# An attention and feed-forward kernel: bias loads of chunks 1 to 3 issued by GpSimd instead of the sync engine

## The chip, the cores and the metric

The kernel runs on one core of a Trainium2 chip. The metric is device time in microseconds for one launch. A core has a matrix engine (TensorE, PE in the profile; its weight loads are PEld), VectorE (DVE), ScalarE (ACT), GpSimd (POOL) and a sync engine (SP) that only issues transfers. Each engine works off its own instructions in program order and waits on semaphores for the others. Transfers between HBM and on-chip memory are started by an instruction on SP, ACT or POOL and then run on 16 shared transfer engines.

## What is computed

Attention with a learned position bias for 4 batches, 8 heads, 576 positions and head size 64, then a layer norm and a feed-forward block of width 2048 on the concatenated heads:

```python
scores = scale * np.matmul(q, k.transpose(0, 1, 3, 2))
x = (psi_rel / psi_i)[..., None]            # from positions alone
bias = np.maximum(x @ w1 + b1, 0.0) @ w2    # one 576 x 576 map per head
scores = scores + bias.transpose(2, 0, 1)[None, :, :, :]
attn = softmax(scores);  a = np.matmul(attn, v)       # heads side by side
xn = (a - mu) / np.sqrt(var + 1e-06) * g_ln
out = a + np.maximum(xn @ w_ch1, 0.0) @ w_ch2
```

## The kernel before, in words

The 576 query positions are cut into four chunks of 128 rows (c = 0 to 3) and a tail of 64 (c = 4). One **unit** is the attention of one batch, one chunk and one head (in a tail unit, two heads); there are 144 units, in the order of the list `ORD` (line 213). That list keeps units of one chunk together, since the four batches share a chunk's bias: chunk 0 up to unit 39, tails in units 40 to 47, chunk 1 in units 48 to 79, chunk 2 in 80 to 111, chunk 3 in 112 to 143.

The bias is computed on the chip in 36 groups of 16 positions (`bias_relu`, `bias_mm`), copied by ScalarE into a tile `ev`, and written to a buffer in HBM, `nb0` to `nb4`, one for each chunk (line 211). The writes of the first twelve groups (the tail and chunk 0) go out on POOL, those of the other 24 on SP. Once all groups of a chunk are written, eight tiles `ldb` of 128 x 576, one for each head, are loaded back (line 326); each is then used by all four batches.

A step `u` of the main loop (line 861) runs `softmax1(u)`: VectorE adds bias and scores and finds the row's extreme (L434), ScalarE takes the exponential (L438) and a scaled half-precision copy (L443). `softmax2(u - 1)` makes the rest of that value (L462, L464), and SP issues a transposing transfer of the result `e` into `pt` or `wend` (L470). `qk` makes the scores of two later units on PE (L391), `pv` multiplies the transposed probabilities by the values (L480). Each finished tile goes through a layer norm: VectorE takes mean and variance (L567, L568), POOL the factor `rs` (L569, L570), ScalarE and VectorE the normalized tile (L596, L599), SP transposes it into `xT` (L601). The feed-forward work on PE (L709, L736), with ScalarE's and VectorE's `hh` (L714, L717), is spread between the units so that PE has work at every step.

`issue_loads(u)` (line 277) goes through a list of loads sorted by the unit that needs them, and issues those whose time has come and whose buffer is free by the program's counters. Keys `kf` (L291, 8 buffers) and queries `qf` (L304, L307, 3 buffers) and values `vf` (L313) are issued on POOL, the bias tiles `ldb` (9 buffers) on SP. The lead is set by two numbers for each kind, the offset in the list and `LOOK`:

```python
loads.append((u0 + (g if c == 4 else 2 * g) - 4, "k", (n, b, g)))
loads.append((u0 + 4 * hh - 3, "q", (b, c, hh)))
loads.append((u0 + h, "b", (seg[n], c, h)))
LOOK = {"k": 5, "q": 6, "b": 7, "v": 0}
```

So a bias tile may be loaded seven steps ahead, and a key tile is asked for 9 - 2g steps ahead of its visit's first unit; it is used 2g units into the visit.

The order on each engine is the order in which the program emits instructions, as a scheduler has arranged them. Transfers are counted on semaphores, eight for SP's queue and eight for POOL's, used in turn; a transfer that comes to a semaphore again first waits until the transfer eight before it has landed.

Of the kernel before, what the change touches and what calls it, by code (L numbers as in the profile page):

```python
# [22 lines left out]
def kernel(  # L23
# [13 lines left out]
    V, S, G, T, SY = nc.vector, nc.scalar, nc.gpsimd, nc.tensor, nc.sync  # L37
# [24 lines left out]
    def halves(t):  # L62
# [31 lines left out]
    nbias = [  # L94
        t[0:(128 if c < 4 else 64) * NH * PITCH].rearrange("(i h j) -> i h j", h=NH, j=PITCH)
        [:, :, 16:16 + SEQ] for c, t in enumerate(nflat)
    ]
# [40 lines left out]
    def after(ins, dep):  # L138
        if dep is not None:
            tc.add_manual_dep(ins.ins, dep.ins.name,  # L140
                              mybir.DependencyInfo(mybir.DependencyClass.Sync,
                                                   mybir.DependencyReason.DATA),
                              reason="pace")
# [133 lines left out]
    def issue_loads(u):  # L277
        wait = set()
        for item in list(loads):
# [5 lines left out]
            if kind == "k":  # L285
# [4 lines left out]
                raw = kp.tile([128, 2, HS], F32, tag="k", name="kf")  # L290
# [4 lines left out]
            elif kind == "q":  # L295
                if not qfree[0]:
                    wait.add(kind)
                    continue
                qfree[0] -= 1
                b, c, hh = key  # L300
                raw = qp.tile([128, 512], F32, tag="q", name="qf")
                if c < 4:
                    raw = raw.rearrange("p (a b) -> p a b", a=4)
                    ld = G.dma_start(out=raw, in_=q_main[b, c, :, 4 * hh:4 * hh + 4])  # L304
                else:
                    raw = raw.rearrange("p (a b) -> p a b", a=8)
                    ld = G.dma_start(out=raw, in_=q_tail[b])  # L307
                if gate_on[0] and (b, c) != ORD[0]:
                    gate.append(ld)
                qt[key] = raw  # L310
            elif kind == "v":
                raw = vp.tile([128, 640], F32, tag="v", name="vf")
                ld = G.dma_start(out=raw.rearrange("p (a b c) -> p a b c", a=2, b=5),  # L313
                                 in_=v_p[key[0], :, 2 * key[1]:2 * key[1] + 2])
                if ttri:
                    after(ld, ttri[max(ttri)])
                vraw[key] = raw
            else:
                _, c, h = key
                if not bfree[0] or mm_done[0] < gend[c]:  # L320
                    wait.add(kind)
                    continue
                bfree[0] -= 1
                raw = ldp.tile([128, SEQ], F32, tag="ld", name="ldb")
                if c < 4:
                    SY.dma_start(out=raw, in_=nbias[c][:, h, :])
                else:
                    SY.dma_start(out=raw[0:64], in_=nbias[4][:, 2 * h, :])
                    SY.dma_start(out=raw[64:128], in_=nbias[4][:, 2 * h + 1, :])
                bt[key] = raw  # L330
# [478 lines left out]
    for _ in range(2):  # L809
        load_w()  # L810
    issue_loads(-6)
    issue_loads(-5)
    V.memset(mhalf, -0.5)
    V.memset(one_sb, 1.0)
    V.memset(half4, 0.5)
    bias_setup()
    issue_loads(-4)
    for n in range(NP + 1):
        if n < NP:
# [172 lines left out]
```

## Time and profile before

| | us |
|---|---|
| median of 3 runs | 678.46 |
| lowest and highest of the runs | 678.29 and 684.29 |
| the profiled execution, whole | 679.99 |
| its span in the profile | 678.2 |
| PE busy | 647.7 (96%) |
| VectorE busy | 457.8 (68%) |
| ScalarE busy | 392.0 (58%) |
| POOL busy | 97.4 (14%) |
| mean granted PE clock | 0.985 of 2.4 GHz |

All times in the rows are microseconds from the start of the span, which is one execution. In rows in order of time the columns are start, duration, engine, line, operation, output<-input, count, and in brackets the idle time just before on that engine and what ended it. "POOLq", "SPq" are the queues of instructions that only issue transfers; a row that merges several (x2, x3) gives the time of them together. A wait for several semaphores is put down to the one that came last.

### The profile page before, as it was taken

To read this page: it belongs to the slowest core of one execution; us is meant where nothing else is said; L and a number is where in the kernel's file an instruction comes from. 1 tells how busy PE (TensorE), PEld (TensorE's weight loads), DVE (VectorE), ACT (ScalarE), POOL (GpSimd) and SP (SyncE) were. 2 spreads that over 40 slices of the span, in tenths; PEclk is the share of its full clock that TensorE was granted. 3 is DMA by queue.
4 is the path that set the end of the run, shared out by engine and by line. 5 is a ranking of instruction groups with operands and counts; after the bars stand their busy time and mean duration, and the time that the engine had idled before them with its cause. 6 is when DMAs were issued, how large, how long until landed. Compare 5 with 4: busy or idle time off the path is not lost.

```text
span 678.2 us, 19142 instructions
## 1 busy us (share of the span) xinstructions
PE 647.7 (96%) x7929; PEld 448.4 (66%) x7929; DVE 457.8 (68%) x1061; ACT 392.0 (58%) x777; POOL 97.4 (14%) x163
## 2 busy tenths in 40 slices
PE   6889996998999889999899999999999999999997
PEld 4447774676466666666667766666776677677775
DVE  6588999778757567686766575757576676766322
ACT  5565847478957447787764577576554455444110
POOL 5312321011000011111101110111011120000000
PEclk9989997899999999999899999999999999999999
DMA  8999885444659996868869789789996976744100
GB/s 312 294 404 331 307 294 161 143 91 115 143 122 148 223 246 156 173 156 164 172 149 239 134 183 181 136 197 181 201 200 144 166 153 125 121 98 87 33 16 17
DMA packets 186955, 117.24 MB, mean 173 GB/s; under 512 B 163956, under 2 KB 164084, under 8 KB 186868
## 3 DMA queue, kind: packets, MB, share of 16 engines
q1 hardware_dynamic: 177124, 81.00, 55.8%
q0 software_dynamic: 9600, 34.84, 16.6%
q8 instruction: 62, 1.02, 0.6%
q10 hardware_dynamic: 144, 0.18, 0.1%
q14 instruction: 25, 0.20, 0.1%
HBM read 60.51 MB, written 15.63 MB: 112 GB/s over the span
## 4 chain that ended last, share of the span: by engine, by line
PE 50%; DVE 0%; ACT 0%; issue 0%
PE hps L709 19%; PE y L736 18%; PE sps L391 6%; PE xps L480 6%; PE bps L181 1%; DVE v L369 0%; DVE x L747 0%; DVE e L462 0%; ACT e L443 0%; DVE x L516 0%; ACT t L438 0%; DVE e L464 0%
## 5 line engine op out<-in xcount | busy, mean ns | idle before, releaser
L709 PE MATMUL hps<-xT,w 128*128 128x128 f16 x3240 | 196.4, 220 | 5.8 <-DVE hh L717 2.6
L709 PEld LDWEIGHTS <-w 128*128 128x128 f16 x3240 | 184.6, 98 | 11.5 <-issue 5.2
L736 PE MATMUL y<-w,hh 128*128 128x512 f16 x810 | 189.1, 381 | 1.9 <-ACT hh L714 1.8
L438 ACT ACTIVATE t<-t,m 128x576 f32<-128x576 f32 x144 | 111.0, 771 | 132.8 <-DVE m L434 132.2
L736 PEld LDWEIGHTS <-hh 128*128 128x128 f16 x864 | 79.7, 98 | 90.6 <-ACT hh L714 3.3
L462 DVE SCALAR_TENSOR_TENSOR e<-t,e 128x512 f16<-128x512 f32 x120 | 82.8, 690 | 81.8 <-ACT e L443 81.5
L434 DVE CUSTOM_DVE_ANT_0 t<-sps,ldb 128x576 f32<-128x576 f32 x144 | 105.9, 753 | 31.4 <-PE sps L391 21.2
L391 PE MATMUL sps<-kf,qf 64*128 64x288 f32 (+1 forms) x640 | 96.6, 436 | 3.5 <-DVE m L434 3.5
L443 ACT ACTIVATE e<-t 128x576 f16<-128x576 f32 x120 | 80.8, 679 | 9.8 <-DMA pt<-e 3.5
L714 ACT ACTIVATE hh<-hps 128x512 f16<-128x512 f32 x72 | 42.0, 583 | 53.4 <-PE hps L709 47.9
L717 DVE SCALAR_TENSOR_TENSOR hh<-hps,hh 128x512 f16<-128x512 f32 x72 | 49.4, 687 | 34.0 <-ACT hh L714 33.5
L391 PEld LDWEIGHTS sps<-kf,qf 64*128 64x128 f32 (+1 forms) x640 | 48.2, 176 | 35.6 <-issue 17.5
L480 PEld LDWEIGHTS <-pt 128*128 128x128 f16 (+1 forms) x1456 | 49.3, 100 | 30.5 <-issue 24.9
L747 DVE SCALAR_TENSOR_TENSOR x<-y,ycs,x 128x512 f32<-128x512 f32 x58 | 43.4, 748 | 32.2 <-PE y L736 32.0
L480 PE MATMUL xps<-v,pt 128*128 128x64 f16 (+1 forms) x1456 | 59.0, 195 | 1.9 <-DMA pt<-e 1.1
L291 POOL DMA_DIRECT2D kf<-in_k_s_dram x56 | 31.1, 556 | 161.4 <-PE sps L391 114.3
L304 POOL DMA_DIRECT2D qf<-in_q_main_dram x32 | 18.5, 577 | 162.4 <-PE xps L480 82.6
L187 ACT ACTIVATE ev<-bps,cb_sb,par_sb 128x144 f32<-128x144 f32 (+27 forms) x48 | 26.0, 593 | 26.2 <-PE bps L181 26.0
L160 ACT ACTIVATE r<-psi_sb,par_sb 128x448 f32<-128x448 f32 (+23 forms) x72 | 39.7, 614 | 0.0
L569 POOL TENSOR_SCALAR rs<-mv 128x1 f32<-128x1 f32 x18 | 9.9, 549 | 146.3 <-DVE mv L568 138.3
L438 ACT ACTIVATION_READ_ACCUMULATOR t<-t,m 128x1 f32 x144 | 27.0, 188 | 0.0
L181 PE MATMUL bps<-r,nw_sb 128*32 128x448 f32 (+24 forms) x200 | 26.9, 494 | 0.0
(121 smaller groups left out, 641.4 us busy)
## 6 DMA issues: line engine op xcount, KB each, us to landing
kf<-in_k_s_dram POOLq DMA_DIRECT2D x56, 288.0 KB, 4.8
w<-in_w_ch_dram SPq DMA_DIRECT2D x22, 512.0 KB, 8.7
ldb<-nb SPq DMA_DIRECT2D x32, 288.0 KB, 4.5
qf<-in_q_main_dram POOLq DMA_DIRECT2D x32, 256.0 KB, 4.6
nb<-ev SPq DMA_DIRECT2D x24, 296.0 KB, 3.4
vf<-in_v_p_dram POOLq DMA_DIRECT2D x16, 320.0 KB, 7.5
out_dram<-x SPq DMA_DIRECT2D x18, 256.0 KB, 2.1
wend<-in_w_ch_dram SPq DMA_DIRECT2D x8, 512.0 KB, 4.8
```

Of the source, the lines that this page charges most:

```text
L160: S.activation(r[:, 0:n], psi_sb[:, 0:n], AF.Relu, bias=pr_sb[:, g4:g4 + 1], scale=1.0)
L391: m = T.matmul(out=o, lhsT=l, rhs=kk, start=True, stop=True, tile_position=(64 * hf, 64 * e))
L434: ttri[u] = V.tensor_tensor_reduce(out=halves(t), in0=ps[:, :, 0:HS], in1=halves(bias), scale=-0.125, scalar=3e38, op0=ALU.add, op1=ALU.mi ...
L438: S.activation(t, t, AF.Exp, bias=m, scale=-1.0, accum_out=l8[b, c][:, h:h + 1])
L443: S.activation(e16[:, 0:SEQ], t, AF.Copy, scale=E_SCALE)
L462: V.scalar_tensor_tensor(out=e16[:, 640:1152], in0=t[:, 0:512], scalar=E_SCALE, in1=e16[:, 0:512], op0=ALU.mult, op1=ALU.subtract)
L480: T.matmul(out=o, lhsT=p[:, m], rhs=v[:, j, a, :], start=(i == 0), stop=(i == len(ops) - 1))
L709: T.matmul(out=h[:, idx * n:idx * n + n], lhsT=w[:, wo + kk * 128:wo + kk * 128 + 128], rhs=xT[k][:, xo + kk, 0:n], start=(i == 0), stop=( ...
L714: S.activation(hh[:, 0], h, AF.Relu)
L717: V.scalar_tensor_tensor(out=hh[:, 1], in0=h, scalar=0.0, in1=hh[:, 0], op0=ALU.max, op1=ALU.subtract)
L736: T.matmul(out=yps[k][t], lhsT=hh[:, a, o:o + 128], rhs=w[:, wo:wo + 512], start=(f == f0 and i == 0), stop=(f == f1 - 1 and i == 2))
L747: V.scalar_tensor_tensor(out=x, in0=y, scalar=ycs[:, g:g + 1], in1=x, op0=ALU.mult, op1=ALU.add)
```

## The change

One line of `issue_loads`: which engine issues the load of a bias tile of chunks 1 to 3. Chunk 0's and the tails' stay on SP.

```diff
@@ issue_loads, kind "b"
                 raw = ldp.tile([128, SEQ], F32, tag="ld", name="ldb")
                 if c < 4:
-                    SY.dma_start(out=raw, in_=nbias[c][:, h, :])
+                    (G if c else SY).dma_start(out=raw, in_=nbias[c][:, h, :])
                 else:
                     SY.dma_start(out=raw[0:64], in_=nbias[4][:, 2 * h, :])
                     SY.dma_start(out=raw[64:128], in_=nbias[4][:, 2 * h + 1, :])
```

24 loads change their queue, eight for each chunk. PE, VectorE and ScalarE keep their instructions and their order. Below are the places where SP's and POOL's rows change. On SP, at chunk 1 (`nb_125` is that chunk's buffer in HBM; the first row is its last write; rows with - stand only in the kernel before):

```order
 L211 DMA nb_125<-ev 16x8x592
-L326 DMA ldb<-nb_125 128x576 x3
 L470 DMA_TRANSPOSE wend<-e_3098 128x9x128
 L470 DMA_TRANSPOSE pt<-e_3137 128x9x128
-L326 DMA ldb<-nb_125 128x576 x2
 L470 DMA_TRANSPOSE pt<-e_3223 128x9x128
 L470 DMA_TRANSPOSE pt<-e_3265 128x9x128
 L751 DMA out_dram<-x 128x512
-L326 DMA ldb<-nb_125 128x576 x2
 L470 DMA_TRANSPOSE pt<-e_3360 128x9x128
 L470 DMA_TRANSPOSE wend<-e_3423 128x9x128
```

The eight loads go, and the transposes follow the write directly. On POOL, at the same place, the rows with + stand only in the changed kernel:

```order
 L304 DMA qf<-in_q_main_dram 128x512
-L291 DMA kf<-in_k_s_dram 128x576 x3
+L291 DMA kf<-in_k_s_dram 128x576 x2
+L326 DMA ldb<-nb_125 128x576 x5
+L291 DMA kf<-in_k_s_dram 128x576
 L304 DMA qf<-in_q_main_dram 128x512
 L291 DMA kf<-in_k_s_dram 128x576
+L326 DMA ldb<-nb_125 128x576 x2
 L569 TENSOR_SCALAR rs<-mv 128x1
 L570 TENSOR_TENSOR rs<-rs,mhalf 128x1
+L326 DMA ldb<-nb_125 128x576
 L304 DMA qf<-in_q_main_dram 128x512
```

Five loads stand ahead of the third key load, two ahead of the layer norm's `rs`, one behind it. At chunks 2 and 3 it is four, then a query load, then three, `rs`, and one. The rows of POOL at chunk 1 again, with what each waits for (DMAHW and DMASW are the semaphores of SP's and of POOL's transfers, eight each):

```order
+L326 DMA ldb<-nb_125 128x576 [waits DMAHW3_49,DMAHW5_49,DMAHW1_49,DMAHW7_49,DMASW7_49,DVE_49]
+L326 DMA ldb<-nb_125 128x576 [waits DMAHW6_49,DMASW0_49,DVE_49]
+L326 DMA ldb<-nb_125 128x576 [waits DMAHW4_49,DMASW1_49,DVE_49]
+L326 DMA ldb<-nb_125 128x576 [waits DMAHW0_49,DMASW2_49,DVE_49]
+L326 DMA ldb<-nb_125 128x576 [waits DMASW3_49,DVE_49]
+L291 DMA kf<-in_k_s_dram 128x576 [waits DMASW4_49,PE_49]
+L304 DMA qf<-in_q_main_dram 128x512 [waits DMASW5_49,PE_49]
+L291 DMA kf<-in_k_s_dram 128x576 [waits DMASW6_49]
+L326 DMA ldb<-nb_125 128x576 [waits DMAHW2_49,DMASW7_49,DVE_49]
```

The first bias load waits for the writes of its chunk, and the sixth uses the same semaphore (DMASW7) as the first, so it waits until the first has landed.

## Rows read from the trace of the kernel before

**Rows 1.** Busy time, share of the span and instructions of each engine.

```profile
PE 647.7 (96%) x7929; PEld 448.4 (66%) x7929; DVE 457.8 (68%) x1061; ACT 392.0 (58%) x777; POOL 97.4 (14%) x163
```

**Rows 2.** Stretches: length, busy (count) PE, PEld, DVE, ACT, POOL; clock, DMA share, GB/s.

```profile
232.00:255.00 23.00, 20.74 (x359) 15.05 (x352) 14.81 (x37) 11.17 (x23) 2.45 (x4) 1.00 1.15 225
255.00:330.00 75.00, 75.00 (x978) 51.04 (x978) 52.53 (x126) 57.49 (x119) 10.93 (x18) 1.00 0.77 168
330.00:340.00 10.00, 8.00 (x113) 6.30 (x110) 8.77 (x19) 7.21 (x13) 2.11 (x3) 0.83 0.83 148
340.00:620.00 280.00, 280.00 (x3606) 196.44 (x3605) 185.41 (x434) 158.78 (x313) 33.74 (x55) 1.00 0.80 160
```

**Rows 3.** PE in order of time, 216 to 260 us: the rows after idle time.

```profile
225.41 2.84 PE L709 MATMUL hps<-xT,w 128*128 128x128 f16 x48 [1.28 <-DVE hh L717]
...
236.10 0.63 PE L480 MATMUL xps<-v,wend 128*64 128x64 f16 x28 [0.53 <-DMA wend<-e]
...
250.19 2.17 PE L709 MATMUL hps<-xT,w 128*128 128x128 f16 x36 [1.30 <-DVE hh L717]
...
253.47 0.63 PE L480 MATMUL xps<-v,pt 128*64 128x64 f16 x28 [0.43 <-DVE x L543]
```

**Rows 4.** SP's queue in order of time: chunk 1's last bias write on; chunk 2.

```profile
223.53 0.58 SPq L211 DMA_DIRECT2D nb<-ev  x1
228.76 1.28 SPq L326 DMA_DIRECT2D ldb<-nb  x3
230.21 2.01 SPq L470 DMA_TRANSPOSE wend<-e  x1
232.39 2.62 SPq L470 DMA_TRANSPOSE pt<-e  x1
...
353.73 1.29 SPq L326 DMA_DIRECT2D ldb<-nb  x3
```

**Rows 5.** SP's waits between 221 and 256 us: total, times, longest.

```profile
SPq L326 <- DMA nb<-ev: 4.6, 1, 4.6
```

**Rows 6.** VectorE and ScalarE in order of time, the same place.

```profile
224.53 0.22 DVE L464 SCALAR_TENSOR_TENSOR e<-t,e 128x64 f16<-128x64 f32 x1
...
228.94 0.22 DVE L464 SCALAR_TENSOR_TENSOR e<-t,e 128x64 f16<-128x64 f32 x1
...
232.64 0.75 DVE L434 CUSTOM_DVE_ANT_0 t<-sps,ldb 128x576 f32<-128x576 f32 x1
...
236.14 0.68 ACT L443 ACTIVATE e<-t 128x576 f16<-128x576 f32 x1 [2.51 <-DMA wend<-e]
...
249.46 0.68 DVE L717 SCALAR_TENSOR_TENSOR hh<-hps,hh 128x512 f16<-128x512 f32 x1
```

**Rows 7.** Transposes of line 470 between 224 and 255 us: issue to landing.

```profile
DMA to landing us min/median/max: 4.2/5.3/6.7
```

**Rows 8.** POOL in order of time, 216 to 242 us: a key load and rs.

```profile
223.73 0.54 POOL L291 DMA_DIRECT2D kf<-in_k_s_dram  x1 [6.52 <-PE sps L391]
...
239.41 0.71 POOL L569 TENSOR_SCALAR rs<-mv 128x1 f32<-128x1 f32 x1 [14.07 <-DVE mv L568]
```

**Rows 9.** Key loads on POOL, whole span: duration of one, ns min/median/max.

```profile
L291 POOL DMA_DIRECT2D kf<-in_k_s_dram x56: 538/538/792, 1.3 to 558.2; - x56
```

**Rows 10.** Transfers by line: count, KB each, median us from issue to landing.

```profile
kf<-in_k_s_dram POOLq DMA_DIRECT2D x56, 288.0 KB, 4.8
...
ldb<-nb SPq DMA_DIRECT2D x32, 288.0 KB, 4.5
```

**Rows 11.** Bias loads on SP, whole span: issuing time, ns min/median/max.

```profile
L326 SPq DMA_DIRECT2D ldb<-nb x32: 319/408/1381, 54.5 to 499.2; - x32
```

**Rows 12.** VectorE's first read of chunk 1's bias, unit 48.

```profile
250.72 0.75 DVE L434 CUSTOM_DVE_ANT_0 t<-sps,ldb 128x576 f32<-128x576 f32 x1
```

**Rows 13.** VectorE at chunk 2's loads: unit 77, and the layer norm's mv.

```profile
365.38 0.75 DVE L434 CUSTOM_DVE_ANT_0 t<-sps,ldb 128x576 f32<-128x576 f32 x1
...
368.45 0.17 DVE L568 BATCH_NORM_AGGREGATE mv<-bs 128x2 f32<-128x6 f32 x1
```

## The prediction

> **What bounds the kernel now.** I read the page's busy times first, then stretches of the span, then the rows in which the matrix engine PE waits, and from there back to whoever was late. PE is busy for 647.7 of 678.2 us [rows 1]. The stretches show where the rest is lost: PE is never idle from 255 to 330 us or from 340 to 620 us, while 2.26 us are missing between 232 and 255 us and 2.00 us between 330 and 340 us [rows 2]. So a change can shorten the run only where PE waits, and a PE that starts later or earlier after 255 us carries that shift to the end.
>
> The bias loads that the change moves are issued in three places, chunk 1's from 228.76 us on, chunk 2's from 353.73 [rows 4], chunk 3's up to 499.2 [rows 11]. The last two places lie inside the stretch without an idle microsecond [rows 2]. Only chunk 1 matters for a gain. There PE waits four times [rows 3]: 1.28 us at 225.41, 0.53 us at 236.10 for a transpose into wend, 1.30 us at 250.19 for VectorE's hh, and 0.43 us at 253.47 for VectorE's x. The last three are the 2.26 us.
>
> Who made those three late? On the sync queue (SP) the last write of chunk 1's bias leaves at 223.53, and the next instruction is the first bias load, which needs that write in HBM. SP waits 4.6 us for it [rows 5] and issues three loads at 228.76; only then come the transposes [rows 4]. The first transpose's input was ready when L464 ended, 224.53 + 0.22 = 224.75 us [rows 6]; it is issued at 230.21, that is 5.46 us late. It takes a median of 5.3 us to land in this stretch [rows 7], and it is what PE waits for at 236.10. ScalarE waits 2.51 us for the same transpose, because it needs the buffer being read [rows 6]; VectorE follows ScalarE, and its hh at 249.46 is what PE waits for at 250.19. The wait at 225.41 began before the bias write was issued, so the change can't reach it.
>
> **The change, part by part.** Leaving SP: 24 loads, each a median of 0.408 us of issuing [rows 11], 9.8 us in all, and with them the wait for the bias writes. SP is off PE's path except through its transposes. In chunk 1 the wend transpose can go at about 224.8 instead of 230.2; with the stretch's 5.3 us it lands at 230.1, and PE, which arrives at 236.10 - 0.53 = 235.57, finds it there: 0.53 us gained. ScalarE's 2.51 us go too, and the second transpose moves up by 3.2 us: its input is ready at 228.94 + 0.22 = 229.16 [rows 6], and it is issued at 232.39 now [rows 4]. VectorE's chain to hh is then some 2.5 us earlier while PE is 0.53 us earlier, so the margin grows by 2 us, more than the 1.30 us wait: all of it is gained. The 0.43 us may go the same way, but that x waits behind two further head steps on VectorE and I don't count it. Bounds: 0 if the transposes land no sooner, 2.26 if all three waits go. I take 0.53 + 1.30 = 1.83 us, since both waits lead back to the same late transposes.
>
> Arriving on POOL: 24 instructions. No bias load of this kind stands there now; the nearest row is the key load, the same 128 x 576 tile, 0.538 us in its shortest and median case and 0.792 at most [rows 9]. So 24 x 0.54 = 12.9 us (19.0 at the longest) on an engine that is busy 97.4 of 678.2 us [rows 1]; its idle time covers that. Landing is about the same, 4.8 us for the key load against 4.5 for the bias load [rows 10]. The first bias tile would land near 228.8 + 4.8 = 233.6 and is first read at 250.72 [rows 12], 17 us later. The bytes in flight are the same: 24 x 288 KB change queues.
>
> The wait for the bias write moves to POOL, and what is queued behind it are one key load, a query load and a key load. The key load goes at 223.73 now [rows 8]; behind five bias loads it goes at about 228.8 + 5 x 0.54 = 231.5, 7.8 us later. It is asked for 8 to 9 steps before its first use; a step lasts 3.95 us (from 250.72, unit 48, to 365.38, unit 77 [rows 12, 13]), so over 31 us of lead stand against 7.8 us of delay and 4.8 of landing. Nothing else waits for it, so I cost it at nothing; without that lead it would be the whole 7.8 us.
>
> Also behind them on POOL stands the layer norm's rs, which ScalarE needs. In chunk 1 the sixth and seventh bias loads come just ahead of it. They need tail buffers, the later of which is free when VectorE's step at 232.64 ends, at 233.4 [rows 6], and the ninth software load waits until the first has landed, 233.6 by the median. They are through by about 234.7; rs starts at 239.41 now [rows 8] and 2.5 us earlier if VectorE gains that. Margin 2.2 us at least. In chunk 2 three loads precede rs; the last needs the buffer that the step at 365.38 frees at 366.13, so it is done at about 366.8, and rs waits for L568, done at 368.62 [rows 13]: margin 1.8 us. The eighth load stands behind rs and holds the next query load for about 1 us, against many steps of lead. If the cover in chunk 2 or 3 were gone, each microsecond of rs beyond 1.8 would delay ScalarE by as much.
>
> What of POOL being slow while VectorE works? VectorE is busy 68% of the span [rows 1], and yet half of 56 key loads take the shortest time and none over 0.792 us [rows 9]. The Trainium skill ("SBUF — State Buffer", "SBUF: two separate sides") speaks against this change: some VectorE operations lock GpSimd out of a shared port, its descriptors are then not written, and loads should be issued from SP; it gives 620 ns growing to about 3100. The trace shows no such growth. By that figure, as an estimate, 24 loads would take 74 us of POOL.
>
> The sum: 678.2 - 1.83 = 676.4 us of span. The profiled execution took 679.99 us, 1.53 above the median of 678.46; taken against itself it would be 678.2, and against the median 678.46 - 1.83 = **676.6 us**.
>
> **The rivals.** *No gain.* The transposes are late because the transfer engines are full, not because SP stands still: their share is 1.15 between 232 and 255 us, the highest of these stretches [rows 2], and the loads only change the queue. Against it: the first transpose is issued 5.46 us late, and that is SP's doing. Time: 678.5. The Trainium skill ("DMA: Bandwidth & Descriptors", "Issuing engines are not separate DMA queues") says just this: loads from several engines share the same 16 engines, and only issuing time is saved. The full share of rows 2 agrees with the first half; SP's 4.6 us is a wait and no issuing time, which the rule doesn't speak of.
>
> *Slower: the burst.* The eight loads now go in one burst: five bias loads, two key loads and a query load between 228.8 and 232.6, 7 x 288 KB + 256 KB = 2.33 MB. Now the key and query loads run from 223.7, while SP stands still. At the stretch's 225 GB/s the burst takes 10.4 us; if transposes got half of the engines meanwhile, a landing would double from 5.3 to 10.6 us. The second transpose is issued 3.2 us earlier, so it decides from a landing of 8.5 us on; at 10.6 it lands 2.1 us later than now, ScalarE and PE wait for it: 678.46 + 2.1 = 680.6. For it: the full share. Against it: the longest landing in this busy stretch is 6.7 us [rows 7].
>
> *Stretched loads on POOL.* Should each load on POOL lose the length of one VectorE step, 0.75 us [rows 12], then the three loads ahead of rs in chunk 2 end 2.25 us later, 0.45 us beyond the margin; so in chunk 3, which has the same order. With both on PE's path: 676.6 + 2 x 0.45 = 677.5. Rows 9 speak against it. This is the lock-out of the Trainium skill's page in this kernel's terms.
>
> *A larger gain.* The stop at 333 us goes too: 2.00 us idle and a clock of 0.83 over the ten microseconds around it, 10 x 0.17 = 1.7 us [rows 2]. But the whole program reaches that place with the same relative order, shifted; nothing of the change is near. 676.6 - 3.7 = 672.9.
>
> **How the numbers follow.** The forecast 0.49, no gain 0.27, the burst 0.11, stretched loads 0.03, larger gain 0.10. The likeliest case spans 676.2 to 677.9 (2.26 and 0.53 us gained). The range takes in no gain with half a microsecond of scatter and most of the way to either outer case: 674.5 to 680.0. A difference of 1%, 6.8 us, is about the least that a measurement here can tell from none; every case above lies inside it. Faster by over 1% needs 671.7, beyond even the larger gain: 0.02. Slower by over 1% needs 685.2, a new stop of PE of some 7 us, or several: 0.04. Within 1%: 0.94.
>
> **What would show it.** Right: SP issues the wend transpose near 225 us; PE's waits at 236 and 250 are gone and it is full from about 226 to 330 us; five loads of 0.54 us on POOL from 228.8; rs no later than now; chunks 2 and 3 as full as before. Wrong: ScalarE still waiting for transposes with landings above 8.5 us (the burst); POOL's loads well over 0.8 us; ScalarE waiting for rs; PE waits of the same size whose releaser is unchanged (no gain); or a PE idle at 330 us that grows by what was gained before it.

## The result, and the profile after

The changed kernel takes a median of 690.28 us against 679.57 us of the kernel before in the same comparison: a ratio of **1.0131 [1.0101, 1.0162]**. A second comparison gave 689.18 against 681.08, 1.0147 [1.0106, 1.0188]. Forecast were 676.6 us, in a range from 674.5 to 680.0, and "within 1%". The change makes the kernel slower by 1.3 to 1.5%, some 8 to 11 us. A ratio here is formed from the fast runs of both kernels and is not that of the two medians, which would be 1.0158 in the first comparison; the kernel before spread from 677.96 to 684.29 us in it. (The kernel before had medians between 679.6 and 682.3 us in the later comparisons, so ratios are used below.)

The profiled execution of the changed kernel took 690.27 us (span 688.5). Busy times of the page, to be held against [rows 1]:

```profile
PE 652.4 (95%) x7929; PEld 449.4 (65%) x7929; DVE 457.8 (66%) x1061; ACT 391.8 (57%) x777; POOL 110.4 (16%) x187
```

POOL gained 13.0 us, the 12.9 that were forecast. The stretches of [rows 2], in the same columns (length, busy of PE, PEld, DVE, ACT, POOL, then clock, DMA share, GB/s):

```profile
232.00:255.00 23.00, 17.86 (x297) 13.03 (x295) 10.57 (x26) 7.68 (x15) 6.60 (x12) 0.92 1.11 168
255.00:330.00 75.00, 74.19 (x974) 50.09 (x974) 53.73 (x128) 54.94 (x114) 11.47 (x19) 0.96 0.89 175
330.00:340.00 10.00, 10.00 (x102) 5.49 (x98) 6.50 (x18) 8.57 (x19) 1.14 (x2) 1.00 0.75 182
340.00:620.00 280.00, 279.05 (x3612) 195.77 (x3610) 187.07 (x435) 160.28 (x316) 42.66 (x72) 1.00 0.83 164
```

From 340 us on PE is all but full, as before. (The changed kernel is 5.6 us late when it comes to the moved loads, and 11 to 12 us late behind them, so equal times are not equal places of the program.) Between 232 and 255 us PE stands still for 5.14 us instead of 2.26, and the bytes moved there fall from 225 to 168 GB/s although the DMA share stays (1.15, now 1.11). PE's rows after idle time in chunk 1, for [rows 3]:

```profile
231.00 2.84 PE L709 MATMUL hps<-xT,w 128*128 128x128 f16 x48 [1.65 <-DVE hh L717]
253.53 0.96 PE L480 MATMUL xps<-v,pt 128*64 128x64 f16 x28 [4.63 <-DMA pt<-e]
255.81 5.28 PE L736 MATMUL y<-w,hh 128*128 128x512 f16 x12 [1.32 <-DVE x L747]
```

The waits at 236 and 250 us are gone, as forecast. In their place PE waits 4.63 us for one transpose. SP's queue, and POOL's, at that place:

```profile
228.36 0.58 SPq L211 DMA_DIRECT2D nb<-ev  x1
229.11 1.48 SPq L470 DMA_TRANSPOSE wend<-e  x1
230.76 14.44 SPq L470 DMA_TRANSPOSE pt<-e  x3
...
245.99 9.61 SPq L470 DMA_TRANSPOSE pt<-e  x1
```

```profile
232.70 2.65 POOL L326 DMA_DIRECT2D ldb<-nb  x5 [10.32 <-DVE m L434]
235.35 0.54 POOL L291 DMA_DIRECT2D kf<-in_k_s_dram  x1
235.88 0.54 POOL L304 DMA_DIRECT2D qf<-in_q_main_dram  x1
236.51 0.54 POOL L291 DMA_DIRECT2D kf<-in_k_s_dram  x1
238.63 1.20 POOL L326 DMA_DIRECT2D ldb<-nb  x2 [1.58 <-DVE m L434]
242.53 0.70 POOL L569 TENSOR_SCALAR rs<-mv 128x1 f32<-128x1 f32 x1 [2.70 <-DVE mv L568]
```

SP issues the wend transpose 0.75 us after the bias write began to be issued, and it lands after 4.1 us; the wait for the write has left SP. But then three transposes, with the pauses between them, take 14.44 us to issue and the next one 9.61, where one took 2.01 and 2.62 [rows 4]. They stand still while POOL's ten loads, issued from 232.70 to 239.83, are on their way. The loads are late themselves: the first three land after 3.4 to 4.4 us, the last two after more than 17, and the two key loads among them, of a kind that lands after 4.8 us in the median before [rows 10], as follows:

```profile
DMA to landing us min/median/max: 14.2/15.9/17.6
```

From 232.70 to 253.50 us, where PE's wait ends, 171 GB/s are moved, four fifths of it for POOL's queue (q0; SP's is q1; packets, MB, share of the 16 engines):

```profile
q0 software_dynamic: 773, 2.83, 67.9%
q1 hardware_dynamic: 2774, 0.69, 40.6%
```

Issue to landing of line 470's transposes from 226 to 262 us (minimum, median, maximum), for [rows 7], and the row of ScalarE that waits for one of the late transposes:

```profile
DMA to landing us min/median/max: 4.1/6.6/20.6
```

```profile
253.59 0.72 ACT L596 ACTIVATE x<-u,rs 128x512 f16<-128x512 f32 x1 [11.69 <-DMA pt<-e]
```

And the transfer engines in two-microsecond stretches; the last two columns are DMA share and GB/s:

```profile
246.00:248.00 2.00, 2.00 (x43) 1.96 (x37) 0.00 (x0) 0.00 (x0) 0.00 (x0) 1.00 1.58 105
248.00:250.00 2.00, 0.90 (x17) 0.72 (x13) 0.00 (x0) 0.00 (x0) 0.00 (x0) 1.00 1.18 60
250.00:252.00 2.00, 0.00 (x0) 0.00 (x0) 0.00 (x0) 0.00 (x0) 0.00 (x0) 0.85 1.40 107
```

The engines count as busy and move 60 to 107 GB/s. VectorE and ScalarE have nothing to do from 246 us on; everything waits for a transpose.

**Where the time is lost.** The start of VectorE's L434 of a unit, set against the same row of before, dates a loss. By unit 44, which is as late as the two units before it, the changed kernel is 5.59 us late (237.55 against 231.96); by unit 52 it is 12.35 late: chunk 1 costs **6.8 us**. PE stands for 5.95 us from 232 to 330 us (5.14 + 0.81) instead of 2.26, which is 3.7. Most of the rest is the clock: it falls to 1.2 GHz while PE stands still, the mean granted clock is 0.57 from 250 to 260 us, in which PE is busy for 5.15, and 0.92 from 260 to 270; as an estimate, 5.15 x 0.43 + 10 x 0.08 = 3.0. From unit 66 to 70 some 2.5 us come back: the stop that lies near 333 us in the kernel before [rows 2] lies near 344 here, and PE waits 0.63 us at it (0.20 and 0.43) instead of 2.00, at a clock of 1.00 instead of 0.83:

```profile
344.09 0.61 PE L736 MATMUL y<-w,hh 128*128 128x512 f16 x2 [0.20 <-ACT hh L714]
```

The 5.6 us ahead of unit 44, in which no instruction differs, are looked at below.

### The profile page after: what moved, and what is told of

It is laid out like the page before. It is cut to its first block, busy times and chain, and to the rows that moved or that the text cites. A ratio compares the mean times of both kernels' runs of the same rounds, so it can differ in the third digit from the quotient of the medians.

```text
span 688.5 us, 19167 instructions
## 1 busy us (share of the span) xinstructions
PE 652.4 (95%) x7929; PEld 449.4 (65%) x7929; DVE 457.8 (66%) x1061; ACT 391.8 (57%) x777; POOL 110.4 (16%) x187
## 4 chain that ended last, share of the span: by engine, by line
PE 60%; DMA 4%; DVE 1%; ACT 1%; issue 1%; ACTq 0%
PE y L736 22%; PE hps L709 21%; PE sps L391 8%; PE xps L480 7%; DMA pt<-e 4%; PE bps L181 2%; DVE x L747 0%; ACT t L438 0%; ACT r L160 0%; DVE v L369 0%; ACT e L443 0%; DVE x L599 0%; ACT x L596 0%; DVE t L434 0%; DVE e L462 0%
## 5 line engine op out<-in xcount | busy, mean ns | idle before, releaser
L736 PE MATMUL y<-w,hh 128*128 128x512 f16 x810 | 192.5, 386 | 3.0 <-ACT hh L714 1.5
L709 PEld LDWEIGHTS <-w 128*128 128x128 f16 x3240 | 184.0, 98 | 10.6 <-issue 4.3
L434 DVE CUSTOM_DVE_ANT_0 t<-sps,ldb 128x576 f32<-128x576 f32 x144 | 105.9, 753 | 33.1 <-PE sps L391 22.2
```

Of the source, the lines that this page charges most:

```text
L434: ttri[u] = V.tensor_tensor_reduce(out=halves(t), in0=ps[:, :, 0:HS], in1=halves(bias), scale=-0.125, scalar=3e38, op0=ALU.add, op1=ALU.mi ...
L709: T.matmul(out=h[:, idx * n:idx * n + n], lhsT=w[:, wo + kk * 128:wo + kk * 128 + 128], rhs=xT[k][:, xo + kk, 0:n], start=(i == 0), stop=( ...
L736: T.matmul(out=yps[k][t], lhsT=hh[:, a, o:o + 128], rhs=w[:, wo:wo + 512], start=(f == f0 and i == 0), stop=(f == f1 - 1 and i == 2))
```

## The experiments

The theories: **A**, the transposes of SP's queue are held up by the burst of loads on POOL's queue, in chunk 1 alone; **B**, POOL's instructions behind the moved wait (keys, queries, rs) come late; **C**, part of the difference has nothing to do with the change. "Chunk 1" in the table is the change of the distance to before from unit 44 to unit 52, a negative one a gain; "landing" is the longest transpose of line 470 issued between 224 and 256 us (for the first row 226 to 262, for e1 224 to 258). Both are of one profiled execution.

| kernel | chunk 1, us | landing, us | time against before |
|---|---|---|---|
| changed kernel | +6.8 | 20.6 | 1.0131 [1.0101, 1.0162] |
| the same again | +7.3 | 20.2 | 1.0147 [1.0106, 1.0188] |
| chunk 1's loads alone on POOL | +6.2 | 18.5 | 1.0097 [1.0061, 1.0132] |
| chunks 2 and 3 alone on POOL | -2.0 | - | 1.0001 [0.9977, 1.0026] |
| one load a step, POOL | +4.1 | 18.4 | 1.0114 [1.0077, 1.0151] |
| and one step later, POOL | -1.4 | 14.4 | 1.0001 [0.9974, 1.0027] |
| and three steps later, POOL | -2.4 | 8.2 | 1.0024 [0.999, 1.0057] |
| the same again | +0.4 | 12.8 | 1.0033 [0.9997, 1.0069] |
| three steps later, SP | -1.1 | 12.6 | 0.9988 [0.9968, 1.0008] |
| one load a step, SP | - | - | 0.9967 [0.994, 0.9993] |
| the same again | -2.4 | 8.0 | 0.9984 [0.9956, 1.0012] |

### Chunk 1 alone, and chunks 2 and 3 alone

```diff
-                    (G if c else SY).dma_start(out=raw, in_=nbias[c][:, h, :])
+                    (G if c == 1 else SY).dma_start(out=raw, in_=nbias[c][:, h, :])
```

> Only chunk 1's eight bias loads are issued by GpSimd; those of chunks 2 and 3 stay on SP. Theory A (chunk 1's loads run on the transfer engines at the same time as SP's transposes and the two slow each other): all of the change's loss is here, 5 to 8 us above the kernel before, 685 to 690 us by the median, with transposes near 235 us that take 10 us or more to land. Theory B (the loads on GpSimd hold up what stands behind them there, the key and query loads and the layer norm's rs, in each of the three chunks): a third of the loss, 2 to 3 us, 681 to 683 us. Theory C (the loss is the early slow clock between 40 and 55 us, chance or a shift of timing, and has nothing to do with where the loads are): as often 684 as 678, like the kernel before.

Measured: 1.0097 [1.0061, 1.0132]. PE's wait and the transposes' landing are close to those of the changed kernel (18.5 us at the longest):

```profile
249.20 0.96 PE L480 MATMUL xps<-v,pt 128*64 128x64 f16 x28 [3.96 <-DMA pt<-e]
```

```diff
-                    (G if c else SY).dma_start(out=raw, in_=nbias[c][:, h, :])
+                    (G if c > 1 else SY).dma_start(out=raw, in_=nbias[c][:, h, :])
```

> Only the bias loads of chunks 2 and 3 are issued by GpSimd; chunk 1's stay on SP. Theory A: no difference, within 1 us of the kernel before, since PE has work throughout there and the loads come in fours and threes, each waiting for a buffer, and not eight at once; no wait of PE near 355 or 485 us. Theory B: two thirds of the loss, 4 to 6 us, with waits for rs or for keys near 370 and 495 us. Theory C: like the kernel before, as often 684 as 678.

Measured: 1.0001 [0.9977, 1.0026]; sixteen of the 24 loads on POOL cost nothing that a quarter of a per cent would show. That is not because transposes are left alone there. Their landing between 340 and 390 us, in this kernel and then in the kernel before:

```profile
DMA to landing us min/median/max: 3.3/6.3/12.1
```

```profile
DMA to landing us min/median/max: 3.2/3.3/5.8
```

It doubles, but PE has work until they arrive (278.5 of the 280 us from 340 on). So the loss is chunk 1's, and theory B, which would hold in all three chunks, falls; in the changed kernel's rows above rs waits for VectorE's mv, not for the loads. In this kernel chunk 1 is that of the kernel before, and still its profiled execution loses 0.42 us there, not 2.26:

```profile
232.00:255.00 23.00, 22.58 (x372) 15.78 (x371) 16.81 (x42) 11.37 (x25) 2.44 (x4) 1.00 1.14 231
```

So the table's column has a scatter of some 2 us, and the waits of [rows 3] are not there in every execution.

### One load a step

```diff
+                if not bfree[0] or mm_done[0] < gend[c] or (0 < c < 4 and nb1[0]):
...
+                    ld = (G if c else SY).dma_start(out=raw, in_=nbias[c][:, h, :])
+                    if c:
+                        nb1[0] += 1
+                        after(ld, ttri[max(ttri)])
```

> All 24 loads on GpSimd as in the change, but at most one for each step of the main loop, each waiting for that step's L434 on VectorE, so that five do not leave together at chunk 1. Theory A: the overlap gets thinner, one load of 288 KB for every 4 us instead of 2.3 MB in 4 us; transposes land in under 9 us and the loss at chunk 1 falls to under 3 us: 678 to 682 us. Theory B: as slow as the change or slower, since eight waits now stand on GpSimd ahead of the keys and rs: 686 to 692 us. Theory C: nothing moves against the change, 688 to 691.

Measured: 1.0114 [1.0077, 1.0151], so no gain. The edit didn't do what it was made for: the steps whose loads it spreads had run by the time the bias write landed. POOL's queue at that place starts and ends so:

```profile
231.06 0.54 POOL L329 DMA_DIRECT2D ldb<-nb  x1 [11.16 <-DVE m L440]
...
237.06 0.54 POOL L329 DMA_DIRECT2D ldb<-nb  x1 [0.41 <-issue]
```

Eight loads in 6.5 us (in the changed kernel the first eight took 4.4), and transposes that land after up to 18.4 us. The same edit with everything on SP:

```diff
-                    ld = (G if c else SY).dma_start(out=raw, in_=nbias[c][:, h, :])
+                    ld = (SY if c else SY).dma_start(out=raw, in_=nbias[c][:, h, :])
```

> All loads on SP as in the kernel before, but at most one for each step, each waiting for that step's L434. The step of the prediction that is tried here: SP's wait for the bias write makes the transposes late, and PE's 2.26 us near chunk 1 come from that. SP still waits for the write before the first load, but sends one load ahead of the transposes instead of three. If the lateness alone counts, PE's waits near 236 and 250 us shrink by 0.5 to 1.5 us: 677 to 678 us where the kernel before has 678.4. If the loads' place among the transposes does not matter: no difference.

Measured: 0.9967 [0.994, 0.9993].

### Thinner in earnest

Each bias load of chunks 1 to 3 is also asked for later, first by three steps:

```diff
-                loads.append((u0 + h, "b", (seg[n], c, h)))
+                loads.append((u0 + h + (3 if 0 < c < 4 else 0), "b", (seg[n], c, h)))
...
+                    ld = (G if c else SY).dma_start(out=raw, in_=nbias[c][:, h, :]); c and after(ld, ttri[max(ttri)])
```

> The changed kernel, but each bias load of chunks 1 to 3 is asked for three steps later and waits for VectorE's L434 of the step that asks for it, so that POOL issues about one a step (two or three steps pass for five of them) and the key and query loads go ahead of them. In the run that asked for one load a step but not later, eight loads still left within 6 us. Theory A (a burst of loads on POOL's queue holds up the transposes of SP's queue; it is the burst that costs, not the queue): the transposes behind chunk 1's last bias write land in 8 us or less, PE's waits on them at 250 us are gone, and the time is that of the kernel before or a little less, 0.995 to 1.001 of it. Rival C (any mixing of POOL's loads with SP's transposes costs, however thin): the loss stays, 1.007 or more, with transposes landing in 12 us or more.

Measured: 1.0024 [0.999, 1.0057]. The profiled execution is what theory A asks for, PE without a gap and 230 GB/s again:

```profile
232.00:255.00 23.00, 23.00 (x375) 16.05 (x374) 17.39 (x41) 12.81 (x27) 5.65 (x10) 1.00 1.19 230
```

But the ratio lies above the 1.001 that A allowed and below the 1.007 of the other theory (its "C" is not the C above), so the kernel ran once more:

> The thin version on POOL once more, for a second profile and more runs: the first gave 1.0024 [0.999, 1.0057], while its profiled execution (679 us) showed PE full from 232 to 330 us and 4.3 us gained between units 44 and 142. Its runs lie in two groups, near 678 and near 685 to 689. Theory A says the second group has a stop at a place that the change does not touch or one where POOL's loads still meet transposes; if this profile falls in it, the rows show which. Expected ratio 0.998 to 1.004; if thin loads on POOL still cost in chunk 1, the profile shows PE waits for transposes between 230 and 280 us.

Measured: 1.0033 [0.9997, 1.0069]. This execution shows small waits all through chunk 1:

```profile
232.00:255.00 23.00, 20.64 (x337) 14.74 (x335) 15.40 (x36) 9.46 (x20) 5.56 (x10) 1.00 1.20 175
```

```profile
DMA to landing us min/median/max: 4.7/7.6/12.8
```

The 12.8 us, however, are not the bias loads' doing. They are the wend transpose's, issued at 224.80 while POOL issued a key, a query and another key load (224.37 to 225.99); POOL's first bias load follows at 234.34. In the kernel before, SP still waits for the bias write while these three loads run, and they have landed (230.10) when the wend transpose is issued at 230.21. On SP, with the same lateness (`SY` in the place of `(G if c else SY)`):

> The kernel before with the same thinning, everything on SP as it was: each bias load of chunks 1 to 3 asked for three steps later and behind that step's L434. The wait for the bias write leaves SP's queue as in the changed kernel, since transposes stand ahead of the loads. Theory A, and the prediction's own step (SP's wait for the write cost 0.53 + 1.30 us of PE's time): PE waits of 236 and 250 us gone, 0.995 to 0.999 of the kernel before, as the earlier one-load-a-step version on SP gave 0.9967. If the queue by itself were worth something, the version with POOL would be faster than this one by over 1 us; theory A says within 1 us.

Measured: 0.9988 [0.9968, 1.0008]. The longest landing, 12.6 us, is again the wend transpose's beside the key and query loads, with no bias load near, and PE waits 0.53 us for it, as in the kernel before. In the same comparison the ratio is 1.0024 on POOL, some 2.5 us more, so theory A's "within 1 us" is not borne out; but the two intervals overlap, and what thin loads on POOL would cost there is not shown. Between the two sizes of burst, one step later instead of three:

```diff
-                loads.append((u0 + h, "b", (seg[n], c, h)))
+                loads.append((u0 + h + (1 if 0 < c < 4 else 0), "b", (seg[n], c, h)))
```

> Between the one-load-a-step version (eight POOL loads within 6 us, loss in chunk 1 of 4.2 us) and the thin one (three loads ahead of the bias loads, gain of 3.7 us there): each bias load of chunks 1 to 3 is asked for one step later and waits for that step's L434. POOL's order at chunk 1 becomes one bias load, a query load, a key load, then three bias loads. Theory A (what costs is the number of loads on POOL's queue that are in flight beside the transposes): transposes land in 8 to 14 us at the longest, PE waits there for 0 to 3 us, and the time lies between the two, 1.000 to 1.008. If the burst didn't matter, the time would be that of the changed kernel, 1.010 or more, or of the kernel before, with transposes as short as 6.7 us.

Measured: 1.0001 [0.9974, 1.0027]. Four loads leave from 230.5 to 232.6 us; the longest landing is 14.4 us, and yet PE loses little:

```profile
250.60 2.17 PE L709 MATMUL hps<-xT,w 128*128 128x128 f16 x36 [0.47 <-DVE hh L717]
```

So a burst of half the size costs no more than the kernel before loses at this place, and the whole burst costs 4 to 7 us (the column of the table).

### What is chance

> The changed kernel once more, unaltered, for a second profile. In the first profile 6.0 us of the loss came in chunk 1 and 4.2 us before any changed instruction had run, where TensorE's granted clock stood at 0.50 for 10 us instead of 3.4. Theory A says that the early part is scatter and no effect of the change: it should differ here (unit 8 begins anywhere between 0 and 4 us later than in the kernel before), while the loss between units 44 and 46 is there again, 4 to 7 us. If the early part comes with this kernel, unit 8 is 4 us late again. Time 1.007 to 1.014 of the kernel before.

Measured: 1.0147 [1.0106, 1.0188]. Unit 8 begins 1.26 us later than in the profile of before (first profile: 4.16), unit 44 2.17 us later (5.59): the early part is scatter, theory C. Between units 44 and 52 7.3 us are lost again (7.5 by unit 46, a little over the 4 to 7 expected, as the ratio is a little over 1.014), at the same wait:

```profile
251.67 0.96 PE L480 MATMUL xps<-v,pt 128*64 128x64 f16 x28 [6.19 <-DMA pt<-e]
```

```profile
250.00:260.00 10.00, 7.01 (x74) 3.52 (x76) 6.17 (x15) 4.20 (x8) 1.22 (x3) 0.66 1.06 212
```

By the end it is 7.7 us late: 2.2 + 7.3 and then 1.75 back by unit 80. That is near the 8.1 us between the medians.

### The disputed cost by itself

> This kernel leaves out the whole computation and writes zeros; it only moves tiles, in seven phases that are separated by waits: (1) eight transposes of 128x1152 half-precision tiles issued by SP, alone; (2) eight loads of 128x576 tiles issued by POOL, alone; (3) both at once, transposes on SP and loads on POOL; (4) both at once, all on SP, in turn; (5) transposes on SP, loads on ScalarE's queue; (6) as (3) again; (7) the loads on POOL alone while VectorE runs sixteen operations on whole tiles. From rows of the kernel before, a transpose takes SP about 2 us to issue and lands after 4.2 us, a key load takes POOL 0.54 us and lands after 4.8: phase 1 about 8 x 2 + 4 = 20 us, phase 2 about 8 x 0.54 + 5 = 9 us. Theory A (transposes of SP's queue and loads of POOL's queue cost each other throughput, beyond sharing it): phases 3 and 6 last longer than phases 1 and 2 together, 35 us or more, phase 4 does not (25 us or less); phase 5 tells whether any second queue does it or POOL's alone. Rival (the engines are only shared, and the loss in the kernel comes from the order in which the pieces wait for each other): phases 3 to 6 each last no longer than 29 us, the sum. Phase 7: if VectorE's work held up POOL's issuing, a load would take POOL well over 0.8 us there; the rows of the changed kernel (0.54 to 0.63 us) say it stays at 0.54.

The phases are 1 to 16, 16 to 25, 25 to 49 (both, POOL), 49 to 69 (both, SP), 69 to 90 (ScalarE's queue), 90 to 112 (both, POOL again), 114 to 125 us (VectorE). Columns: length, busy DVE, busy POOL, clock, DMA share, GB/s:

```profile
2.00:16.00 14.00, 2.85 (x12) 0.00 (x0) 1.00 0.89 169
16.00:25.20 9.20, 1.23 (x8) 4.36 (x8) 1.00 0.73 257
25.20:49.00 23.80, 1.96 (x16) 4.23 (x8) 1.00 1.02 198
49.00:68.60 19.60, 2.50 (x17) 0.00 (x0) 1.00 1.06 241
68.60:90.10 21.50, 1.93 (x16) 0.00 (x0) 1.00 1.03 220
...
114.00:125.00 11.00, 9.55 (x22) 4.24 (x8) 1.00 0.62 215
```

Theory A's 35 us are wrong: both queues at once take 23.8 us, hardly more than one after the other (14.0 + 9.2). Taken in turn on one queue they need 19.6. What the phases show instead is who waits. Alone, a transpose lands every 1.4 us; beside the eight loads the second lands only when the loads are through, 16 us after the start (25.20 to 41.20), and the other six then come quickly. The loads last longer too: the eighth lands after 15.8 us, against 9.0 alone. With the loads on ScalarE's queue the second transpose lands after 12.1 us. The last phase: POOL takes 4.24 us for eight loads, 0.53 each, beside a VectorE that is busy for 9.55 of 11 us.

> Leaves out the whole computation and writes zeros; six phases separated by waits. Earlier: eight transposes alone take 13.6 us, landing 1.4 us apart; eight loads on POOL alone take 9.1; both together 23.7, and the first two transposes land 7.4 and 15.9 us after the start, the other six then 1.4 apart. Phases: (1) 8 transposes on SP with 2 loads on POOL, (2) with 4 loads, (3) with 8 loads, each waiting until the one before has landed, (4) 8 plain loads on SP with 8 loads on POOL, no transpose, (5) transposes on ScalarE's queue and 8 loads on SP, (6) 8 plain loads on SP alone. Theory A (transposes wait behind the burst of another queue): the landing of the second transpose grows with the number of loads, about 5 us with 2 and 8 with 4, against 15.9 with 8; in phase 3 the transposes come no more than 3 us apart; phase 5 as with SP and POOL swapped, the second transpose after 12 us or more. If two queues by themselves were the cause, phase 4's SP loads would starve as well, the second landing after 10 us or more and the phase longer than 9.1 us plus phase 6; if it is the transposes' small packets, phase 4's two queues take turns and the second SP load lands within 6 us.

With two loads on POOL the second transpose is read 5.9 us after the first was issued (2.04), with four 11.2 us after (16.74). The later phases ran into each other, since the wait between them did not cover all loads, and are left aside.

The same with phases that wait for every transfer of the one before:

```python
PH = (("load", 8, G, SY), ("trans", 8, SY, S), ("trans", 2, G, SY), ("trans", 4, G, SY), ("trans", 8, G, SY))
# kind, number of plain loads, their queue, the other queue
```

> Leaves out the whole computation and writes zeros; five phases, each begun only when every transfer of the one before has landed (in the earlier kernel of this kind loads of one phase ran into the next two). (1) 8 plain loads on SP with 8 plain loads on POOL, (2) 8 transposes on ScalarE's queue with 8 loads on SP, (3) 8 transposes on SP with 2 loads on POOL, (4) with 4, (5) with 8. Eight loads on one queue alone took 9.1 to 9.9 us; transposes with 8 loads on POOL came 7.4, 15.9 and 16.8 us after the start. Theory A, in the form that transposes wait behind a burst of plain loads of another queue: phase 1's two queues take turns, its second SP load lands within 6 us and it ends within 16 us; phase 2 is like phase 5, the second transpose after 10 us or more; the second transpose of phases 3, 4 and 5 after about 6, 11 and 16 us. If two queues by themselves were the cause, phase 1's first SP loads would land after 10 us or more. If it is POOL's queue, phase 2's second transpose lands within 7 us.

The phases begin at 0.7, 16.5, 40.6, 55.3 and 74.7 us; the row of each is VectorE's first touch of the second tile of the second queue, and the stretches are the phases:

```profile
4.34 0.15 DVE L79 COPY acc<-lx 128x1 f32<-128x1 f32 x1 [0.50 <-DMA lx<-in_k_s_dram]
...
31.04 0.15 DVE L79 CAST acc<-pt 128x1 f32<-128x1 f16 x1 [6.14 <-DMA pt<-e]
...
47.15 0.15 DVE L79 CAST acc<-pt 128x1 f32<-128x1 f16 x1 [0.62 <-DMA pt<-e]
...
66.75 0.15 DVE L79 CAST acc<-pt 128x1 f32<-128x1 f16 x1 [3.98 <-DMA pt<-e]
...
93.85 0.15 DVE L79 CAST acc<-pt 128x1 f32<-128x1 f16 x1 [14.13 <-DMA pt<-e]
```

```profile
0.70:16.50 15.80, 4.16 (x21) 4.38 (x8) 1.00 0.82 299
16.50:40.60 24.10, 2.30 (x19) 0.00 (x0) 1.00 1.06 196
...
74.70:101.50 26.80, 1.86 (x16) 4.25 (x8) 1.00 1.07 187
```

Plain loads on two queues don't starve each other: 299 GB/s are moved, and the last loads of SP and of POOL land at 16.16 and 15.06 us, about together. (The second load on SP lands 3.6 us after the start, as theory A asked, but SP had issued it at 1.20, ahead of POOL's first load at 1.27, so it decides little.) Transposes do, on ScalarE's queue beside loads on SP (14.5 us) as on SP beside POOL: the second after 6.5 us with two loads, 11.5 with four, 19.2 with eight. Theory A holds in this form: **a transpose waits for nearly the whole burst of plain loads that another queue has put up, in each of the three pairs of queues tried.** The burst lasts longer beside transposes as well: the eight loads of the last phase land after 4.2 to 14.8 us (3.3 to 5.1 alone).

### A version better than both

> The kernel before with at most one bias load a step, each behind that step's L434, all on SP: the candidate for a version better than both. It gave 0.9967 [0.994, 0.9993]; the wait for the bias write no longer stands ahead of the transposes. Expected 0.994 to 1.000 again, and PE waits of 236 and 250 us gone.

Measured: 0.9984 [0.9956, 1.0012], after 0.9967 [0.994, 0.9993]. One bias load stands ahead of the transposes instead of three, and PE has no gap from 232 to 255 us. (The expectation has it wrong that the wait for the write is gone from there: the write leaves at 226.04, and the load that waits for it still precedes the wend transpose.)

```profile
230.04 0.33 SPq L329 DMA_DIRECT2D ldb<-nb  x1
230.54 2.13 SPq L476 DMA_TRANSPOSE wend<-e  x1
```

```profile
232.00:255.00 23.00, 23.00 (x375) 16.01 (x374) 17.94 (x44) 12.81 (x27) 2.44 (x4) 1.00 1.16 233
```

By its medians it is 1.5 to 2 us faster than the kernel before, which is at the limit of what these comparisons can tell, and no run sets it apart from the versions near 1.000; it is clearly faster than the changed kernel.

## Why the prediction was wrong

**What bounds the kernel, and where.** Right. Chunk 1 alone decides, chunks 2 and 3 are free (1.0001), and a shift made there reaches the end but for the 1.75 to 2.5 us that come back at the stop of 333 us.

**The gain of 1.83 us.** Half right. The order is as forecast: SP issues the transposes right behind the write. In the changed kernel the first lands in 4.1 us and PE's wait for it is gone; those behind it then don't move. Where nothing runs over the gain, PE has no gap left (23.00 of 23 us, one load a step on SP and three steps later on POOL, 2.4 us less than in the profile of before). But the waits of [rows 3] were taken from one execution, and another with the same chunk 1 lost only 0.42 us. Nor is an early issue an early landing: with the same key and query loads of POOL beside it, the wend transpose took 8.2, 12.8 and 12.6 us in the three profiles of the versions three steps later, where 5.3 was counted. How much of the lateness was SP's wait stays open, since the version without a gap on SP keeps that wait ahead of the transposes. (The wait at 225.41 began at 224.13, and so 0.6 us after the bias write was issued and not before it, as the prediction has it. The change didn't remove it all the same: it is 1.65 us in the changed kernel.) The versions on SP, which keep the gain without the loss, are worth 0.1 to 0.3%, with one interval of three that leaves out 1: some 1 to 2 us at most.

**POOL's cost.** Right. 24 loads added 13.0 us of busy time (12.9 forecast), for which PE does not wait. Duration of a bias load on POOL over the whole span (ns, minimum, median, maximum):

```profile
L326 POOL DMA_DIRECT2D ldb<-nb x24: 536/536/629, 232.7 to 509.4; - x24
```

The rival of stretched loads is out. The rule that was cited for it (the Trainium skill, "SBUF — State Buffer", "SBUF: two separate sides") did not show itself: no load came near its 3100 ns, and beside a VectorE busy for 87% of a phase a load took 0.53 us. That does not refute it, since its figure is for a copy on VectorE, and no copy of a whole tile ran beside the 24 loads or in that phase.

**Keys, queries and rs.** Right: no wait of PE on them, though the key loads behind the first five bias loads landed after 14.2 and 17.6 us and not 4.8, and rs waits for mv.

**The step that failed** is in the change's first accounting: "Landing is about the same", "The bytes in flight are the same: 24 x 288 KB change queues". It takes a load for the same load on any queue, and so puts the transposes' 5.3 us beside it at no change. On SP's queue a load stands in line with the transposes and is taken in turn, 241 GB/s for the two kinds together. From another queue both run at once, at 187 to 220 GB/s: the transposes get the smaller part and wait for the burst, and the burst itself is late. In the changed kernel a bias load landed after up to 17.4 us instead of 4.5 to 4.8, a transpose after up to 20.6 instead of 5.3, PE waited 4.63 us for one of these, and chunk 1 lost 6.8 us where 1.83 were to be gained.

**The burst rival was the right place with the wrong size.** It counted the first eight loads and their 2.33 MB rightly (two more bias loads followed within 2 us) and asked for 10.4 us and a landing of 10.6, priced at 2.1 us and given 0.11. Measured were landings of 18 to 21 us and a loss of 6 to 7 us, which is beyond every case that the prediction priced. Sharing half and half at a constant 225 GB/s was the mis-sized term: SP's queue got 0.69 of 3.52 MB, a fifth, and 171 GB/s were moved in all. Its point of decision, 8.5 us, was not right either: with a longest landing of 14.4 us the kernel with the half burst still lost nothing (1.0001); it matters which transpose is late. The price also left out the clock, which by the estimate above took 2 to 3 us beside PE's stop of 4.6 to 6.2 us.

**What spoke against it was read wrongly.** "The longest landing in this busy stretch is 6.7 us" [rows 7] came from a stretch in which POOL's key, query and key load had landed (230.10) before the first transpose was issued (230.21), and after which POOL issued one load at a time; it says next to nothing on a burst. The trace of before had a better witness, some 20 us earlier, where one query load and one transpose meet:

```profile
209.39 5.07 SPq L601 DMA_TRANSPOSE xT<-x  x1
```

```profile
DMA to landing us min/median/max: 9.6/9.6/9.6
```

```profile
214.00:216.00 2.00, 2.00 (x27) 0.67 (x24) 1.44 (x4) 0.69 (x2) 0.00 (x0) 1.00 1.07 50
```

A transpose that takes 5.07 us to issue and 9.6 to land, beside a query load that takes 8.5, and 50 GB/s at a DMA share of 1.07: what the changed kernel shows in large. The prediction looked at medians and at the stretch with the waits.

**No gain.** Its rule, that loads from several engines share the same engines and only issuing time is saved (the Trainium skill, "DMA: Bandwidth & Descriptors", "Issuing engines are not separate DMA queues"), holds for plain loads, 299 GB/s on two queues. For transposes the measurement decides against it: eight loads from another engine put the second transpose off to 16 to 19 us after the start. The same page says ("Queues, rings and completion order") that each transfer engine takes the queues in turn, a packet at a time. That fits an order in which short packets come off badly; it alone does not say why eight loads and two transposes need 19 us, and no run here settles that.

**A larger gain.** The stop at 333 us shrank in the changed kernel, and 1.75 to 2.5 us came back. But its first wait, 1.57 us in the kernel before, was 0.29 with chunks 2 and 3 alone on POOL, 2.06 with chunk 1 alone and 2.52 in one execution of the version three steps later: it scatters, and that the change did anything to it is not shown.

## What to carry to other kernels

Before moving a transfer to another queue, look at what the old queue carries beside it: here loads that stood in line with transposes cost little, and the same loads in a burst on another queue held the transposes for nearly as long as the burst lasted. Count the loads that will be in flight together, and look for a place in the trace where such a pair already meets, at its longest landing and its GB/s, not at medians. If the aim is to free a queue of a wait, the waiting instruction can also go behind the urgent ones in the same queue, as in the version three steps later on SP; that lost nothing (0.9988), but gained nothing certain either. And ask what the wait kept apart: without it, SP's transposes met the key and query loads of POOL.

## What the runs showed of the hardware

- A DMA share above 1 says nothing of throughput: 60 GB/s at 1.18 in the changed kernel, 50 at 1.07 in the kernel before, 299 at 0.82 with plain loads on two queues.
- Issuing is held up along with the transfer: a transpose of line 470 takes SP 1.3 to 3.3 us to issue in the kernel before (218 to 256 us), and in the changed kernel 9.61 where an earlier one stands still, so what is behind it on SP comes late as well.
- A burst of plain loads and a few transposes from two queues slow each other: eight loads alone landed after 3.3 to 5.1 us, beside transposes after 4.2 to 14.8; the second transpose after 6.5, 11.5 and 19.2 us with two, four and eight loads.
- In PE's stops of 4.63 and 6.19 us the granted clock fell to the 1.2 GHz level; from 250 to 260 us, in which the stops end and PE works again, it was 0.57 and 0.66 of 2.4 GHz in the mean, which by the estimate above added 2 to 3 us to the stop's own length.
